# Head of a fused layernorm, state-space and SwiGLU kernel: other queues for the first loads, gate matmuls by halves of K

## The chip, the cores and the metric

The kernel runs on one core of one Trainium2 chip. The metric is the device time of one execution in microseconds; for several runs the median is given. A core has five engines that run their own instruction streams and meet at semaphores: TensorE (PE, matrix multiplications into the accumulator memory PSUM), VectorE (DVE), ScalarE (ACT), GpSimd (POOL) and SyncE (SP). Transfers between device memory and on-chip memory are done by 16 DMA engines. Here they are issued from two queues, SyncE's and ScalarE's.

## The reference

The input x has 2048 rows of 512 values in bfloat16. Each row is normalized to mean 0 and variance 1, and the result feeds two branches that are added to x:

```python
xn = _layernorm(x, axis=-1)
return x + _A_ref(xn, ...) + _B_ref(xn, B_w_gate, B_w_up, B_w_down)

# A: a diagonal complex recurrence along the rows, P = 512 states
dt = exp(log_dt); Lam_bar = exp(dt * Lam)
Bu = xn @ (((Lam_bar - 1) / Lam)[:, None] * Bmat).T
h = Lam_bar * h + Bu[t]                     # for every row t
y = 2 * Re(hseq @ Cmat.T) + xn * Dskip

# B: SwiGLU, F = 1376
(silu(xn @ w_gate) * (xn @ w_up)) @ w_down
```

## The kernel before

The 2048 rows are cut into 16 tiles of 128 rows, and four tiles make a chunk of 512 rows. Matmuls need xn with its columns on the partitions. For chunk 0 that transpose is done by TensorE, tile by tile (`xt_tile_fine`), and ScalarE copies the result from PSUM to `xnT`. Chunks 1 to 3 are transposed by a DMA on SyncE's queue (`xt_chunk_dma`).

For each chunk TensorE does the gate and up projections in pairs of 128-column tiles (`ffn_gate`, `ffn_up`, matmuls in line 713), the state-space input (`ssm_b_chunk`, line 818), and later the down projection together with the output of the recurrence in one accumulation (`dc_chunk`, lines 901 and 914). ScalarE empties PSUM with a silu (line 725) or a plain copy (lines 771 and 825). VectorE multiplies gate and up (line 773) and runs the recurrence (`ssm_elem_chunk`, lines 849 and 858). PSUM has eight banks, handed out in pairs in turn, so a matmul that starts a pair waits until ScalarE or VectorE has emptied it.

Everything is recorded as a task with what it reads and writes. A planner then orders each engine: TensorE's and SyncE's tasks keep the order in which they were recorded, while ScalarE, VectorE and GpSimd take what the planner's estimated durations and priorities make best. So a change in the head can reorder VectorE and ScalarE much later. An `order=` argument ties a task behind another without a wait.

The head works as follows. SyncE's queue loads x tiles 0, 1, 2, a slice of the gate weights (columns 512 to 767, all K), x tile 3, then the up weights, the rest of the gate weights, the rest of the up weights, and x tiles 4 to 7 in one load. ScalarE's queue loads log_dt (1 KB), the gate weights' columns 0 to 511 in two halves of K (`a0` and `a1`), then Lambda_im and Lambda_re (1 KB each). VectorE takes the statistics of a tile (line 466), aggregates them (470), adds epsilon (474); GpSimd raises to the power -1/2 (478); VectorE applies (485). Tile 0 is applied in two halves. TensorE meanwhile runs ten idle matmuls of 512 columns (`pe_warm`, line 450), then transposes tile 0 in two halves (543) with more idle matmuls between and after.

Then `ffn_gate_quarters` computes the gate projection of columns 0 to 767, six tiles in three PSUM pairs, one quarter of the chunk's rows (one x tile) at a time: 24 matmuls of 128 columns per quarter (line 752), each column tile with all four K parts at once, and only the very first one in two halves. The transposes of the next tile come between them. Three small transposes in line 457 turn the parameter rows into columns; they stand after the first eight gate matmuls.

Later SyncE's queue does, one after the other, the DMA transposes of B (real, imaginary), of xn's chunk 1, and of C (real, imaginary), and then loads x tiles 8 to 11, the down weights and the rest. The first transpose waits for all loads issued before it (line 380), and every load recorded after a transpose waits for that transpose. Chunk 2 is normalized on ScalarE (line 495), with a factor computed on VectorE (492).

Of the kernel before, what the change touches and what calls it, by code (L numbers as in the profile page):

```python
# [19 lines left out]
    warm=10,  # L20
# [218 lines left out]
def bass_parallel_sum__ssm_conv_s5__swiglu_ffn__prompt_kernel(  # L239
# [32 lines left out]
    with es:  # L272
# [46 lines left out]
        prow = sb("prow", [4, 3, 128], B16)  # L319
# [45 lines left out]
        def BK(b):  # L365
            return [("bk", b, 0), ("bk", b, 1)]
# [29 lines left out]
        def pload(name, slot, src, order=()):  # L396
            return dma(name, prow[:, slot, :], src.rearrange("(a p) -> a p", p=128), [("prow", slot)], 1024, eng="act", order=order)
        FQ = 4 * 128
        act_q = [pload("ld_ldt", 2, A_log_dt)]
# [6 lines left out]
        act_load("ld_wgA0", wg[:, 0:2, 0:FQ], wg_v[:, 0:2, 0:FQ], [("wg", "a0")], 256 * FQ * 2)  # L406
        dma("ld_x2", x_sb[:, 2:3, :], x_v[:, 2:3, :], [("x", 2)], TILEB)
        act_load("ld_wgA1", wg[:, 2:4, 0:FQ], wg_v[:, 2:4, 0:FQ], [("wg", "a1")], 256 * FQ * 2)
        dma("ld_wg0", wg[:, :, FQ:FH0], wg_v[:, :, FQ:FH0], [("wg", 0)], 512 * (FH0 - FQ) * 2)
        dma("ld_x3", x_sb[:, 3:4, :], x_v[:, 3:4, :], [("x", 3)], TILEB)  # L410
        act_q.append(pload("ld_lim", 1, A_Lambda_im, (act_q[-1],)))
        act_q.append(pload("ld_lre", 0, A_Lambda_re, (act_q[-1],)))
# [41 lines left out]
        def params_t(slot):  # L454
            def tr(e):
                for k in range(3):
                    inst = e.transpose(out=ptr[:, slot, 4 * k:4 * k + 4], in_=prow[0:4, k, :], identity=ident[0:4, 0:4])
                return inst
            g.add("pe", tr, reads=[("prow", k) for k in range(3)] + [("ident",)], writes=BK(slot), name="parT", est=100, ninst=3)
# [21 lines left out]
        def ln_apply(a, parts=1, order=()):  # L481
            w = D // parts
            for h in range(parts):
                cs = slice(h * w, (h + 1) * w)
                last = g.add("dve", lambda e, a=a, cs=cs: e.tensor_scalar(out=xn_sb[:, a % NXN, cs], in0=x_sb[:, a, cs], scalar1=mv[:, a, 0:1], scalar2=rstd[:, a:a + 1],
                                                                          op0=ALU.subtract, op1=ALU.mult),
                             reads=[("x", a), ("mv", a), ("rstd", a)], writes=([("xn", a % NXN)] if h == parts - 1 else []) + ([("xh", h)] if parts > 1 else []),
                             name="xn%d" % a, est=90 + 260 // parts, order=order)
            return last
# [10 lines left out]
        def ln_chunk0():  # L500
            bn_st(0)
            bn_ag(0)
            last = ln_ve(0, 1)
            ln_rstd(0, 1)
            last = ln_apply(0, parts=2, order=(bn_st(1, order=(last,)),))
            last = ln_ve(1, 1, order=(bn_ag(1, order=(last,)),))
            ln_rstd(1, 1)
            return bn_st(2, order=(last,))

        def ln_chunk0_rest(last, par_bank):  # L510
            last = ln_apply(1, order=(last,))
            for a in range(2, 4):
                last = ln_ve(a, 1, order=(bn_ag(a, order=(last,)),))
                hold[a] = ln_rstd(a, 1)
                if a == 2:
                    last = params_ev(par_bank, (last,))
                last = ln_apply(a, order=(bn_st(a + 1, order=(last,)),) if a < 3 else (last,))
# [15 lines left out]
        def xt_tile_fine(a, parts=1, wbank=None):  # L533
            n = KT // parts
            for h in range(parts):
                if h:
                    pe_warm(1, 256, wbank)
                slot = xt_pair[0] + (a + h) % 2

                def tr4(e, h=h, slot=slot):  # L540
                    for j in range(n):
                        kt = h * n + j
                        inst = e.transpose(out=ptr[:, slot, j * 128:(j + 1) * 128],
                                           in_=xn_sb[:, a % NXN, kt * 128:(kt + 1) * 128], identity=ident[:])
                    return inst
                g.add("pe", tr4, reads=([("xn", a % NXN)] if h == parts - 1 else []) + ([("xh", h)] if parts > 1 else []) + [("ident",)], writes=BK(slot), name="xT%d" % a, est=n * 64, ninst=n)

                def evac(e, h=h, slot=slot):
                    return e.activation(out=xnT[:, 0, a % 4, h * n:(h + 1) * n, :],
                                        in_=ptr[:, slot, 0:n * 128].rearrange("p (k t) -> p k t", k=n), func=AF.Identity)  # L550
                g.add("act", evac, reads=BK(slot), writes=([("xnT", 0, a % 4)] if h == parts - 1 else []) + ([("xnT0", h)] if parts > 1 else []), name="xTev%d" % a, est=190 + 310 // parts)
# [26 lines left out]
        def small(eng, name, fn, reads, writes, est=90):  # L578
            g.add(eng, fn, reads=reads, writes=writes, name=name, est=est, prio=_CFG['prio_par'])
# [40 lines left out]
        def params_b():  # L620
            dve_ts("thT", "thn", float(TP), ALU.mult)
            dve_range("thn")
            dve_range("thT")
            for i, n in enumerate(["lre", "lim"]):
                o = S(n)
                small("dve", n, lambda e, o=o, i=i: e.tensor_copy(out=o, in_=praw[:, i, :]), [("praw", i)], R(n))
            dve_tt("lam_re", "r", "cos_thn", ALU.mult)
            dve_tt("lam_im", "r", "sin_thn", ALU.mult)
            dve_ts("lm1", "lam_re", -1.0, ALU.add)
            dve_tt("lre2", "lre", "lre", ALU.mult)  # L630
            dve_tt("lim2", "lim", "lim", ALU.mult)
            dve_tt("den", "lre2", "lim2", ALU.add)
            o, a_ = S("rden"), S("den")
            small("dve", "rden", lambda e, o=o, a_=a_: e.reciprocal(out=o, in_=a_), R("den"), R("rden"))
            dve_tt("n1", "lm1", "lre", ALU.mult)
            dve_tt("n2", "lam_im", "lim", ALU.mult)
            dve_tt("n3", "n1", "n2", ALU.add)
            dve_tt("g_re", "n3", "rden", ALU.mult)
            dve_tt("n4", "lam_im", "lre", ALU.mult)
            dve_tt("n5", "lm1", "lim", ALU.mult)  # L640
            dve_tt("n6", "n4", "n5", ALU.subtract)
            dve_tt("g_im", "n6", "rden", ALU.mult)
            dve_ts("s_2gre", "g_re", 2.0, ALU.mult)
            dve_ts("s_m2gim", "g_im", -2.0, ALU.mult)
            dve_ts("s_m2gre", "g_re", -2.0, ALU.mult)
# [10 lines left out]
        def _tables():  # L656
            thn = S("thn")
            for pt in range(PT):
                b = pt % 2
                g.add("act", lambda e, pt=pt, b=b: e.activation(out=tm[:, b, :], in_=iot[:], func=AF.Identity, scale=thn[:, pt:pt + 1]),  # L660
                      reads=R("thn") + [("iot",)], writes=[("tm", b)], name="tm%d" % pt, est=620, prio=_CFG['prio_tab'])
# [35 lines left out]
        def wres(nm, i):  # L697
            if nm == "wg" and i < 4:
                return [("wg", "a0"), ("wg", "a1")]
            return [(nm, 0 if i < 6 else 1)]  # L700
# [34 lines left out]
        def ffn_gate_quarters(pairs, last):  # L735
# [3 lines left out]
            xt_tile_fine(0, parts=2, wbank=banks[pairs[-1]])  # L739
            pe_warm(3, 256, banks[pairs[-1]])  # L740
            tiles = [(2 * ip + k, banks[ip] + k) for ip in pairs for k in range(2)]
            for q in range(4):
                for ii, (i, bk) in enumerate(tiles):
                    if q == 0 and ii == 2:
                        params_t(tiles[-1][1])
                        ln_chunk0_rest(last, tiles[-1][1])
                    if q < 3 and ii == (4 if q == 0 else 2):
                        xt_tile_fine(q + 1)
                    for k0, k1 in (((0, 2), (2, 4)) if q == 0 and ii == 0 else ((0, 4),)):
                        def mm(e, bk=bk, i=i, q=q, k0=k0, k1=k1):  # L750
                            for kt in range(k0, k1):
                                inst = e.matmul(pbank[:, bk, q * 128:(q + 1) * 128], lhsT=wg[:, kt, i * 128:(i + 1) * 128], rhs=xnT[:, 0, q, kt, :],
                                                start=(kt == 0), stop=(kt == KT - 1))
                            return inst
                        xr = [("xnT", 0, q)] if q else [("xnT0", h) for h in range((k1 + 1) // 2)]
                        g.add("pe", mm, reads=wres("wg", i) + xr, writes=BK(bk), name="mm_gq%d_%d" % (i, q), est=(k1 - k0) * 56, ninst=k1 - k0)
# [170 lines left out]
        if _CFG["warm"]:  # L927
            pe_warm(_CFG["warm"])
        ffn_gate_quarters([0, 1, 2], ln_chunk0())
# [106 lines left out]
```

## Time and profile before

The median of four runs is 180.73 us (180.31 to 181.07). The profiled execution took 180.75 us, of which the span from the first to the last instruction is 179.0 us; the 1.75 us around it are outside the profile.

| | TensorE | VectorE | ScalarE | GpSimd |
|---|---|---|---|---|
| busy, us | 174.7 | 160.9 | 86.5 | 12.9 |
| share of the span | 98% | 90% | 48% | 7% |

| moment | us from the span's start |
|---|---|
| first idle matmul | 0.83 |
| statistics of x tile 0 begin | 2.90 |
| first transpose on TensorE | 5.18 |
| first gate matmul | 6.12 |
| first up matmul | 12.97 |
| x tiles 8 to 11, statistics begin | 41.43 |

Times are counted from the span's start. A row of the timeline or of the chain begins with a start and a length in microseconds; "x8" means that eight like instructions were merged. An engine's row can end with the idle time before it and what ended it. In the list of waits three numbers follow the pair: the total, how often, and the longest. "PEld" is the weight load of a matmul, which can run ahead of it.

### The profile page before, as it was taken

The page shows a single profiled execution, that of the slowest core. Times are in us where ns is not written, and L with a number is a line of the kernel's source. Part 1 is how long each engine was busy: PE and PEld are TensorE (multiplying, and loading weights), DVE is VectorE, ACT ScalarE, POOL GpSimd, SP SyncE. Part 2 cuts the span into 40 slices and gives each one's busy share as a digit, 9 for nine tenths or more (in the row PEclk, how much of TensorE's full clock was granted, in tenths as well). Part 3 has the DMA queues.
Part 4 walks back from the last instruction along what each step waited for, and adds up shares of the span by engine and source line. Part 5 has one row for each costly group of instructions (what it writes and reads, how often), then busy time and mean ns, then how long its engine had stood idle before and what let it go on. Part 6 is the DMA issues. An engine that isn't in the chain of part 4 may idle for free.

```text
span 179.0 us, 2380 instructions
## 1 busy us (share of the span) xinstructions
PE 174.7 (98%) x919; PEld 83.6 (47%) x927; DVE 160.9 (90%) x273; ACT 86.5 (48%) x107; POOL 12.9 (7%) x24
## 2 busy tenths in 40 slices
PE   8999999999999999999999999999999999999994
PEld 2694444444434444444444444444444444444743
DVE  3978759987799999999999999999999999999833
ACT  3379899899596992060655651000965620000000
POOL 3361300001400000210000000000000000000000
PEclk9999999999999999999999999999999999999999
DMA  5994546669450000002330000001100000001012
GB/s 153 355 352 89 110 87 126 109 151 359 149 111 10 0 0 0 0 0 89 79 72 0 0 0 4 0 0 59 59 0 4 0 0 0 0 0 62 29 59 88
DMA packets 23410, 12.37 MB, mean 69 GB/s; under 512 B 15112, under 2 KB 23400, under 8 KB 23400
## 3 DMA queue, kind: packets, MB, share of 16 engines
q1 hardware_dynamic: 22832, 11.70, 24.4%
q10 hardware_dynamic: 568, 0.53, 1.0%
q8 instruction: 7, 0.11, 0.3%
q14 instruction: 3, 0.02, 0.0%
HBM read 6.46 MB, written 2.10 MB: 48 GB/s over the span
## 4 chain that ended last, share of the span: by engine, by line
PE 70%; DMA 20%; SPq 2%; ACT 2%; DVE 2%; POOL 1%; issue 1%
PE pb L713 24%; PE pb L901 21%; PE pb L914 15%; PE pb L818 8%; DMA x_sb<-in_A_x_dram 7%; DMA BT<-in_A_B_im_dram 3%; DMA hss<-in_A_C_im_dram 3%; DMA BT<-in_A_B_re_dram 3%; DMA xnT<-xn_sb 2%; DMA hss<-in_A_C_re_dram 2%; SPq L385 2%; ACT xn_sb L495 2%; DVE st L466 1%; PE pb L781 1%; POOL rstd L478 1%
## 5 line engine op out<-in xcount | busy, mean ns | idle before, releaser
L858 DVE TENSOR_TENSOR_SCAN rot<-sm,car,rot 128x512 bf16<-128x512 f32 x32 | 39.0, 1265 | 0.1
L901 PE MATMUL pb<-wd,hT 128*128 128x512 bf16 (+3 forms) x194 | 38.1, 355 | 0.2
L713 PE MATMUL pb<-xnT,wu 128*128 128x512 bf16 x160 | 37.3, 379 | 0.4 <-ACT uf L771 0.4
L713 PE MATMUL pb<-xnT,wg 128*128 128x512 bf16 x136 | 32.0, 379 | 0.0
L914 PE MATMUL pb<-W,hss 128*128 128x512 bf16 (+2 forms) x140 | 28.1, 355 | 0.2
L818 PE MATMUL pb<-xnT,BT 128*128 128x512 bf16 x128 | 28.1, 379 | 0.0
L901 PEld LDWEIGHTS pb<-wd,hT 128*128 128x128 bf16 (+1 forms) x198 | 18.5, 98 | 19.9
L725 ACT ACTIVATE sg<-pb 128x1024 bf16<-128x1024 f32 x20 | 20.2, 1022 | 10.5 <-PE pb L713 10.4
L713 PEld LDWEIGHTS pb<-xnT,wu 128*128 128x128 bf16 x160 | 15.6, 98 | 19.3 <-ACT uf L771 0.9
L771 ACT ACTIVATE uf<-pb 128x1024 bf16<-128x1024 f32 x20 | 20.4, 1022 | 7.0 <-PE pb L713 6.8
L713 PEld LDWEIGHTS pb<-xnT,wg 128*128 128x128 bf16 x136 | 13.2, 98 | 16.4 <-issue 0.8
L914 PEld LDWEIGHTS pb<-W,hss 128*128 128x128 bf16 x144 | 13.5, 98 | 14.3
L818 PEld LDWEIGHTS pb<-xnT,BT 128*128 128x128 bf16 x128 | 12.5, 98 | 15.1
L825 ACT ACTIVATE u_sb<-pb 128x1024 bf16<-128x1024 f32 x16 | 16.3, 1027 | 3.9 <-PE pb L818 3.5
L466 DVE BATCH_NORM_STATS2 st<-x_sb 128x6 f32<-128x512 bf16 x16 | 10.2, 683 | 5.6 <-DMA x_sb<-in_A_x_dram 5.6
L773 DVE TENSOR_TENSOR hT<-sg,uf 128x1024 bf16<-128x1024 bf16 x20 | 13.3, 675 | 2.0 <-ACT uf L771 2.0
L919 DVE TENSOR_TENSOR x_sb<-pb,x_sb 128x512 bf16<-128x512 f32 (+2 forms) x18 | 10.9, 620 | 4.7 <-PE pb L914 4.7
L495 ACT ACTIVATE xn_sb<-x_sb,nmr,rstd 128x512 bf16<-128x512 bf16 x8 | 5.9, 803 | 10.8 <-DVE nmr L492 10.8
L800 ACT ACTIVATE sg<-pb 96x1024 bf16<-96x1024 f32 x2 | 2.0, 1020 | 17.4 <-PE pb L781 17.4
L849 DVE TENSOR_TENSOR rot<-rot,sin 128x2048 bf16<-128x2048 bf16 x8 | 9.7, 1214 | 0.0
L849 DVE TENSOR_TENSOR rot<-u_sb,sin 128x2048 bf16<-128x2048 bf16 x8 | 9.7, 1214 | 0.0
L849 DVE TENSOR_TENSOR rot<-u_sb,cosT 128x2048 bf16<-128x2048 bf16 x8 | 9.7, 1211 | 0.0
(71 smaller groups left out, 139.5 us busy)
## 6 DMA issues: line engine op xcount, KB each, us to landing
out_dram<-x_sb SPq DMA_DIRECT2D x15, 128.0 KB, 1.7
x_sb<-in_A_x_dram SPq DMA_DIRECT2D x3, 512.0 KB, 7.5
wd<-in_B_w_down_dram SPq DMA_DIRECT2D x1, 1280.0 KB, 7.0
wu<-in_B_w_up_dram SPq DMA_DIRECT2D x1, 768.0 KB, 6.2
wg<-in_B_w_gate_dram SPq DMA_DIRECT2D x1, 608.0 KB, 7.5
wu<-in_B_w_up_dram SPq DMA_DIRECT2D x1, 608.0 KB, 8.6
x_sb<-in_A_x_dram SPq DMA_DIRECT2D x4, 128.0 KB, 2.8
wg<-in_B_w_gate_dram ACTq DMA_DIRECT2D x2, 256.0 KB, 3.7
```

Source lines behind the costliest of these rows:

```text
L466: return g.add("dve", lambda e, a=a: e.bn_stats(out=st[:, a, :], in_=x_sb[:, a, :]), reads=[("x", a)], writes=[("st", a)], name="bnst%d" % ...
L713: inst = e.matmul(pbank[0:fs, bk, :].rearrange("p (j t) -> p j t", j=4), lhsT=w[:, kt, i * 128:i * 128 + fs], rhs=xnT[:, c % 2, :, kt, :], ...
L725: g.add("act", lambda e: e.activation(out=sg[rows, sl, 0:n, :].rearrange("p a t -> p (a t)"), in_=pair_f32(rows, bk, 512 * n), func=AF.Sil ...
L771: g.add("act", lambda e: e.activation(out=uf[rows, ul, 0:n, :].rearrange("p a t -> p (a t)"), in_=pair_f32(rows, bk, 512 * n), func=AF.Ide ...
L773: g.add("dve", lambda e: e.tensor_tensor(out=hT[rows, hb, i0:i0 + n, :], in0=sg[rows, sl, 0:n, :], in1=uf[rows, ul, 0:n, :], op=ALU.mult), ...
L818: inst = e.matmul(pbank[:, bk, :].rearrange("p (j t) -> p j t", j=4), lhsT=BT[:, ri, kt, pt * 128:(pt + 1) * 128], rhs=xnT[:, c % 2, :, kt ...
L825: g.add("act", lambda e: e.activation(out=u_sb[:, us].rearrange("p r t -> p (r t)"), in_=pair_f32(slice(0, 128), b0), func=AF.Identity), r ...
L849: tt = lambda out, a, b, op, r, w, nm: g.add("dve", lambda e: e.tensor_tensor(out=out, in0=a, in1=b, op=op), reads=r, writes=w, name="%s_% ...
L858: g.add("dve", lambda e, A0=A0, A1=A1, k=k, ri=ri, pt=pt: e.tensor_tensor_scan(out=A1[:, k, ri, :], data0=rr[:, pt:pt + 1].to_broadcast([1 ...
L901: inst = e.matmul(pbank[:, bk, 0:nc_], lhsT=hT[0:fs, hb, i, lt * 128:(lt + 1) * 128], rhs=wd[0:fs, i, c0:c0 + nc_], start=(i == 0), stop=F ...
L914: inst = e.matmul(pbank[:, bk, 0:nc_], lhsT=hss[:, hb, pt, ri, lt * 128:(lt + 1) * 128], rhs=W12[:, ri, pt, c0:c0 + nc_], start=False, sto ...
L919: g.add("dve", lambda e, bk=bk, a=a, c0=c0, nc_=nc_: e.tensor_tensor(out=x_sb[:, a, c0:c0 + nc_], in0=pbank[:, bk, 0:nc_], in1=x_sb[:, a, ...
```

## The change

On SyncE's queue x tiles 0 to 2 are followed by the two small loads of Lambda_im and Lambda_re and then by x tile 3; the slice of gate weights is gone from it. On ScalarE's queue log_dt is followed by two loads that hold the gate weights' columns 0 to 767, one per half of K. The parameter rows lie in 12 partitions instead of 4 by 3, so that one transpose serves them, and it moves between the two halves of tile 0's transpose.

Ten idle matmuls of 512 columns become 41 of 128. The idle matmul between the halves goes, and the three of 256 columns after them become two of 128. On VectorE the aggregate and epsilon of tile 1 come between the two halves of tile 0. All four tiles are now transposed and copied out in halves, and the gate matmuls run over all six column tiles with the first half of K and then with the second; in the last quarter only the first two tiles are halved. Small parameter work on ScalarE is held behind the last of these copies, and two small copies on VectorE behind the normalization of tile 3.

```diff
-        prow = sb("prow", [4, 3, 128], B16)
+        prow = sb("prow", [12, 128], B16)
...
+        def pload(name, slot, src, eng="sp"):
+            return dma(name, prow[4 * slot:4 * slot + 4, :], src.rearrange("(a p) -> a p", p=128), [("prow", slot)], 1024, eng=eng)
+        act_q = [pload("ld_ldt", 2, A_log_dt, "act")]
...
-        act_load("ld_wgA0", wg[:, 0:2, 0:FQ], wg_v[:, 0:2, 0:FQ], [("wg", "a0")], 256 * FQ * 2)
+        act_load("ld_wgA0", wg[:, 0:2, 0:FH0], wg_v[:, 0:2, 0:FH0], [("wg", "a0")], 256 * FH0 * 2)
         dma("ld_x2", x_sb[:, 2:3, :], x_v[:, 2:3, :], [("x", 2)], TILEB)
-        act_load("ld_wgA1", wg[:, 2:4, 0:FQ], wg_v[:, 2:4, 0:FQ], [("wg", "a1")], 256 * FQ * 2)
-        dma("ld_wg0", wg[:, :, FQ:FH0], wg_v[:, :, FQ:FH0], [("wg", 0)], 512 * (FH0 - FQ) * 2)
+        act_load("ld_wgA1", wg[:, 2:4, 0:FH0], wg_v[:, 2:4, 0:FH0], [("wg", "a1")], 256 * FH0 * 2)
+        pload("ld_lim", 1, A_Lambda_im)
+        pload("ld_lre", 0, A_Lambda_re)
         dma("ld_x3", x_sb[:, 3:4, :], x_v[:, 3:4, :], [("x", 3)], TILEB)
-        act_q.append(pload("ld_lim", 1, A_Lambda_im, (act_q[-1],)))
-        act_q.append(pload("ld_lre", 0, A_Lambda_re, (act_q[-1],)))
...
-                for k in range(3):
-                    inst = e.transpose(out=ptr[:, slot, 4 * k:4 * k + 4], in_=prow[0:4, k, :], identity=ident[0:4, 0:4])
+            g.add("pe", lambda e: e.transpose(out=ptr[:, slot, 0:12], in_=prow[:], identity=ident[0:12, 0:12]),
...
+        def ln_chunk0(par_bank):
+            last = stats(1, hold["last"])
+            last = ln_half(0, 1, order=(last,))
+            last = params_ev(par_bank, (last,))
+            last = bn_st(2, order=(last,))
+            last = ln_apply(1, order=(last,))
...
+            small(...): order=(hold["evac"],) if eng == "act" else ()
...
-            xt_tile_fine(0, parts=2, wbank=banks[pairs[-1]])
-            pe_warm(3, 256, banks[pairs[-1]])
+            pe_warm(41, 128, wbank)
+            ln_first()
+            xt_tile_fine(0, bridge=bridge)      # bridge: params_t, ln_chunk0
+            pe_warm(2, 128, wbank)
             for q in range(4):
+                if q < 3:
+                    steps = [(i, bk, 2 * kh, 2 * kh + 2) for kh in range(2) for i, bk in tiles]
+                else:
+                    steps = [(i, bk, 2 * kh, 2 * kh + 2) for kh in range(2) for i, bk in tiles[:2]] + [(i, bk, 0, 4) for i, bk in tiles[2:]]
+                for n, (i, bk, k0, k1) in enumerate(steps):
+                    if q < 3 and n == 8:
+                        xt_tile_fine(q + 1)
...
-        if _CFG["warm"]:
-            pe_warm(_CFG["warm"])
-        ffn_gate_quarters([0, 1, 2], ln_chunk0())
+        ffn_gate_quarters([0, 1, 2])
```

## The prediction

> **What bounds the kernel now.** I read the busy shares first (TensorE 98%, VectorE 90%), then the chain that ended last, then who waited for whom. TensorE looks like the bound everywhere, so anything saved in its first 13 us should come out at the end. The chain, in order of time (start, length, what), says otherwise:
>
> ```profile
> 4.89 9.36 DMA x_sb<-in_A_x_dram
> ...
> 14.64 4.59 DMA BT<-in_A_B_re_dram
> ...
> 19.25 5.50 DMA BT<-in_A_B_im_dram
> ...
> 24.77 4.25 DMA xnT<-xn_sb
> ...
> 29.04 4.20 DMA hss<-in_A_C_re_dram
> ...
> 33.26 4.60 DMA hss<-in_A_C_im_dram
> ...
> 37.88 3.53 DMA x_sb<-in_A_x_dram
> ...
> 41.43 2.47 DVE st L466 x4
> ...
> 47.01 2.93 ACT xn_sb L495 x4
> 49.94 0.92 ACT uf L771
> ...
> 50.91 8.81 PE pb L713 x40
> ```
>
> Up to 50.9 us the end hangs on SyncE's queue: tiles 4 to 7 of x are the last of the initial loads, the first transpose waits for all of these, five transposes follow one another, then tiles 8 to 11 are loaded, normalized on VectorE, GpSimd and ScalarE, and only then does ScalarE copy out the bank that TensorE wants. From 50.91 on TensorE runs without a wait: 179.0 - 50.9 = 128.1 us. The waits (in total, times, longest) show the meeting point:
>
> ```profile
> PEld pb L713 <- ACT uf L771: 0.9, 1, 0.9
> PE pb L713 <- ACT uf L771: 0.4, 1, 0.4
> ```
>
> TensorE arrives there 0.4 us early. A head that ends earlier only lengthens this wait; one that ends up to 0.4 us later costs nothing. The head itself, TensorE alone:
>
> ```profile
> 5.18 0.37 PE L543 MATMUL pb<-ident,xn_sb 128*128 128x128 bf16 x2
> ...
> 6.12 0.69 PE L752 MATMUL pb<-xnT,wg 128*128 128x128 bf16 x8
> 6.75 0.22 PE L457 MATMUL pb<-ident,prow 4*128 4x4 bf16 x3
> ...
> 8.44 0.62 PE L752 MATMUL pb<-xnT,wg 128*128 128x128 bf16 x8 [0.24 <-ACT xnT L549]
> ...
> 9.12 1.50 PE L752 MATMUL pb<-xnT,wg 128*128 128x128 bf16 x24
> ...
> 12.97 4.26 PE L713 MATMUL pb<-xnT,wu 128*128 128x512 bf16 x19
> ```
>
> From 6.12 to 12.97 are 6.85 us. Spacing is (1.50 - 0.22)/23 = 0.056, so 96 gate matmuls and 12 transposes take 6.05; 0.8 is waits and the parameter transposes.
>
> Last, the load stream in quarter microseconds (TensorE, weight loads, VectorE, ScalarE, GpSimd, clock, DMA share, GB/s), with 512-byte rows (the wg slice) and 1536-byte rows (wu):
>
> ```profile
> 5.50:5.75 0.25, 0.25 (x5) 0.21 (x4) 0.25 (x2) 0.16 (x1) 0.10 (x1) 1.00 1.09 317
> 8.75:9.00 0.25, 0.25 (x8) 0.25 (x6) 0.22 (x3) 0.00 (x0) 0.25 (x1) 1.00 1.08 393
> ```
>
> The engines are full in both; longer rows move more.
>
> **What the Trainium skill says.** "DMA: Bandwidth & Descriptors", section Queues, rings and completion order: each DMA engine takes packets in turn from the queues that have work, so a load on ScalarE's queue shares the engines with SyncE's. The trace agrees that they share, but not evenly in the short run: from 4.00 to 4.25 SyncE's queue moved 0.05 MB and ScalarE's 0.02, from 4.75 to 5.00 0.00 and 0.08. The same page, Why small descriptors are slow: a fixed overhead per packet; 317 against 393 GB/s agrees. "TensorE: Matmul & The Clock Gate", What's actually happening: the clock rises after about 3.4 us of activity, in a free-running window. Here 512-wide idle matmuls are 0.43 apart, and the clock record has full speed from 5.5, 4.7 us after the first. The same page, Architectural detail: VectorE is strictly in order, so what stands behind a waiting instruction waits too; its order below matters for that.
>
> **Part by part.** *Idle matmuls.* 41 of 128 columns are 5248 columns against 5120: at 0.43 per 512, 4.4 us, ending at 5.2 as before. Nothing, since the first half of tile 0 is normalized only at 5.04. At equal activity the clock should rise at the same time.
>
> *Parameters.* One transpose for three, now between the two halves of tile 0 and so ahead of all gate matmuls. Lambda_im and Lambda_re go from ScalarE's queue to SyncE's, behind x2. On the old queue their last landing events were 0.35 and 0.74 us after that of the load ahead of them (5.90, then 6.25 and 6.64). x2 landed at 1.72 + 3.3 = 5.0; so Lambda_re lands at about 5.75, bounds 5.3 and 6.6. VectorE now does tile 1's aggregate and epsilon between the halves of tile 0, so half two is normalized at 5.6 (before 5.3), which this wait hides. Transposes at 5.8 to 6.0, two idle matmuls, first gate matmul at 6.1, as before. The parameter copy stands on VectorE ahead of x2's statistics: tile 1 is normalized at 7.2 instead of 6.7; its transposes come only after 16 gate matmuls, at 7.3.
>
> *Gate weights.* ScalarE's queue carries 786 KB instead of 524. It had moved its 524 by 5.3 us; 262 KB more take 0.8 us if it gets nearly everything (346 GB/s at 4.75) and 1.55 at half; with the 0.6 from last data to landing seen on the old load, 6.7 to 7.4. I take 7.0. The 12 matmuls on the first K half end at 6.1 + 0.67 = 6.8: a wait of 0.2.
>
> *Halves.* The copy of each tile becomes two (0.38 each, 0.28 apart, against 0.60), and 8 matmuls cover it: 0.45 against 0.53 needed, some 0.08 left per tile; the 0.41 before tile 1's matmuls goes. Sum: 7.0 + 84 x 0.056 + 12 x 0.056 + 0.3 = 12.7. The up projection begins 0.2 us earlier (12.3 to 13.5 over both bounds). TensorE then waits 0.6 instead of 0.4 at 50.9. Worth nothing; without that cover it would be worth the 0.2.
>
> *Load stream.* This moves the end. No bytes change, but 256 KB in 512-byte rows become 1536-byte ones: 262/317 - 262/393 = 0.16 us less. The other 524 KB go from 1024-byte rows (346) to 393: at most 0.18 more, in a stretch where the engines were not yet full, so perhaps nothing. Against it SyncE issues two small loads (0.38 + 0.35) for one slice (0.44), so later issues come 0.3 us later; ScalarE's longer backlog covers that; uncovered it costs 0.3. Net -0.2, bounds -0.34 and +0.3. Every later link shifts by the same.
>
> *Order after.* Built, the changed program has the same TensorE order from the up projection on, and ScalarE still has silu, four normalizations, then the awaited copy. VectorE's order changes: statistics of tiles 8 to 11 now stand ahead of one table operation (0.68) and two scans (1.2 each). It idles for that load with 3.0 us of work behind it, and has hardly a free moment until 169. The last h was ready at 165.6 and is first used at 169.7: 4.1 of margin become about 1.2; W (69.9, used at 76.0) keeps 3. Free as long as this cover holds.
>
> Sum against the profiled execution: 179.0 - 0.2 = 178.8 span; that run took 180.75, the median is 180.73, so 180.5 us. A difference below 0.3% (0.54 us) can hardly be told from no change.
>
> **Rivals.** *Faster, by the loads.* Both row gains come in full (0.34), and the engines' free share from 2.0 to 4.5 us (0.3 us in sum) is filled by ScalarE's longer rows: -0.64, 180.1. For it: shares of 0.66 to 0.78 up to 2.75. [...]
>
> *Slower, by the second K half.* All six tiles wait for it, so the up projection begins at 12.7 + (landing - 7.0), and the end is 179.0 + (that start - 12.97 - 0.42) once the cover at 50.9 is used up: no loss against before up to a landing at 7.7, 0.3% from 8.25. With a third of the stream (320/3 = 107 GB/s) the last 262 KB take 2.45 us: landing at 5.3 + 2.45 + 0.6 = 8.35, up projection at 14.05, +0.66: 181.4. Lambda_re landing past 6.6 would act in the same place. For it: SyncE's queue holds long rows right behind x3. Against it: ScalarE's queue had over half from 2.75 to 5.25.
>
> *Slower, by VectorE.* A lag of over 4.1 us makes the last down projection wait; at 5 it is 181.4. Against: the 3.0 above.
>
> *No cover at 50.9*, the head's whole 0.8 arriving at the end, would need this wait to be absent, and the chain denies it.
>
> **Numbers.** Forecast, end tied to the load stream: 0.60, nearly all of it within 0.3%. Faster by the loads 0.17; late K half 0.13; VectorE 0.06; the rest unknown, 0.04, put to slower. Faster 0.19, same 0.58, slower 0.23. The forecast's own range is 180.4 to 181.0; taking in the nearer part of the outer cases, 180.0 to 181.4.
>
> **What would show it.** Right: x's second load (512 KB) landing within 0.35 us of 14.25 and the awaited L771 copy shifted by as much; up projection between 12.3 and 13.5; wait at L713 on L771 of 0.4 to 1. Wrong: no such wait (the head is late), gate matmuls waiting for the weights beyond 7.7, a cold clock past 6 us, or TensorE waiting for VectorE near 170.

## The result, and the profile after

The changed kernel takes 182.05 us, the median of 43 runs (180.48 to 183.87), against 180.76 for the kernel before (64 runs, 180.23 to 181.46): a ratio of 1.0058, with an interval of 1.0046 to 1.007. That ratio doesn't count the one run at 183.87, far above the others, and isn't one of medians, which would give 1.0071. The changed kernel is slower, where no change was forecast, and the median lies outside the range of 180.0 to 181.4. The profiled execution took 181.48 with a span of 179.7; before, the span was 179.0.

The chain that ended last, after (start, length, what):

```profile
2.60 4.29 DMA prow<-in_A_Lambda_re_dram
...
6.98 0.16 PE pb L453
...
7.48 0.89 PE pb L760 x16
...
13.95 12.09 PE pb L713 x56
...
49.25 1.41 ACT xn_sb L485 x2
50.66 0.92 ACT uf L780
51.62 8.81 PE pb L713 x40
```

Where SyncE's loads and transposes stood, the 1 KB load of Lambda_re now begins the chain, and TensorE's head follows it. The meeting point has moved from 50.91 to 51.62, and these 0.71 us are the whole difference of the spans. The waits after, in the parts that answer to those shown of before (total, times, longest):

```profile
PE pb L453 <- DMA prow<-in_A_Lambda_re_dram: 1.5, 1, 1.5
...
PEld pb L713 <- ACT uf L780: 0.8, 1, 0.8
...
PE pb L713 <- ACT uf L780: 0.3, 1, 0.3
```

The head on TensorE, from the timeline after:

```profile
5.20 0.27 PE L542 MATMUL pb<-ident,xn_sb 128*128 128x128 bf16 x2
6.98 0.16 PE L453 MATMUL pb<-ident,prow 12*128 12x12 bf16 x1 [1.51 <-DMA prow<-in_A_Lambda_re_dram]
...
7.32 1.05 PE L760 MATMUL pb<-xnT,wg 128*128 128x128 bf16 x16
...
11.86 2.09 PE L760 MATMUL pb<-xnT,wg 128*128 128x128 bf16 x32
13.79 2.54 PE L713 MATMUL pb<-xnT,wu 128*128 128x512 bf16 x11
```

The parameter transpose waits 1.51 us for Lambda_re, which lands at 6.89, and every gate matmul is queued behind it. From the first gate matmul to the up projection it is 6.47 us, less than the 6.85 of before; but it starts at 7.32 instead of 6.12, so the up projection starts 0.82 later.

That is not yet all, since a wait at 51 us is left: the other arm is late too. VectorE's and then ScalarE's timeline after:

```profile
15.42 2.47 DVE L461 BATCH_NORM_STATS2 st<-x_sb 128x6 f32<-128x512 bf16 x4 [1.75 <-DMA x_sb<-in_A_x_dram]
...
42.15 2.47 DVE L461 BATCH_NORM_STATS2 st<-x_sb 128x6 f32<-128x512 bf16 x4 [2.53 <-DMA x_sb<-in_A_x_dram]
```

```profile
47.73 2.93 ACT L485 ACTIVATE xn_sb<-x_sb,nmr,rstd 128x512 bf16<-128x512 bf16 x4 [1.69 <-DVE nmr L482]
50.56 1.00 ACT L780 ACTIVATE uf<-pb 128x1024 bf16<-128x1024 f32 x1
```

x tiles 4 to 7 arrive 1.15 us later than before (their last landing event is at 15.40 instead of 14.25), tiles 8 to 11 at 42.15 instead of 41.43 (0.72 later, since the loads and transposes between took 0.43 us less this time), and ScalarE, which from 47.73 on is never idle, comes to the awaited copy 0.71 later. The chain leads from that copy to TensorE because a TensorE event happens to end at 49.25 too; ScalarE's row shows that it was waiting for nothing then. So two arms, each some 0.7 to 0.8 us late, meet at 51.6.

The windows of the load stream after (TensorE, weight loads, VectorE, ScalarE, GpSimd, clock, DMA share, GB/s):

```profile
5.50:5.75 0.25, 0.00 (x0) 0.00 (x0) 0.09 (x1) 0.24 (x1) 0.25 (x1) 1.00 0.88 275
...
8.75:9.00 0.25, 0.25 (x8) 0.24 (x5) 0.25 (x1) 0.25 (x2) 0.25 (x1) 1.00 1.07 389
```

In the first of them TensorE is idle, and VectorE, whose next instruction is the parameters' copy, nearly so. The runs differ in one thing more: in 11 of 43 timed runs the mean granted clock is 0.991, and these took 182.1 to 182.9. In the 184 runs of before that were taken beside the experiments it is 0.999 or more.

Why do two loads of 1 KB take until 6.89? The DMA queues of the changed kernel from 5.0 to 5.5 us (packets, MB, share of 16 engines), in the trace's view of the transfers:

```profile
q10 hardware_dynamic: 112, 0.17, 115.4%
```

This is ScalarE's queue, and SyncE's moved nothing in that half microsecond: x2 had landed at 5.25, Lambda_im and Lambda_re stood next, and the 786 KB of gate weights had the engines.

And why is the end of the x load late? The same view from 12.5 to 14.0 us:

```profile
q1 hardware_dynamic: 256, 0.25, 51.7%
q8 instruction: 1, 0.02, 4.7%
```

One packet of 16 KB of instructions, 4.7% of 24 engine-microseconds or 1.1 us on a single engine. It came at 12.76, while x was still being loaded; before, at 13.44, when the load was nearly done. Of the load's 16 landing events 15 had come by 14.34; the last alone came at 15.40. Three of the experiments below with narrow idle matmuls show the same: 15 events by 14.42, the last at 15.49 to 15.50. Which engine carried the packet is not in the trace, so that it was the late one is inferred. 31 more idle matmuls, each with its weight load, are 62 more instructions on TensorE. "Runtime: NRT & Kernel Launch" of the Trainium skill, section Instruction fetch mechanics, says that instructions are fetched in blocks of 16 KiB, 256 instructions, over a DMA queue, and that this is mostly hidden. The trace agrees with the size; that it is hidden depends on what the engine has to carry at the time.

### The profile page after: what moved, and what is told of

It reads as the page before. It is cut to its first block, busy times and chain, and to the rows that moved or that the text cites. A ratio compares the mean times of both kernels' runs of the same rounds, so it can differ in the third digit from the quotient of the medians.

```text
span 179.7 us, 2438 instructions
## 1 busy us (share of the span) xinstructions
PE 174.3 (97%) x946; PEld 86.2 (48%) x954; DVE 160.3 (89%) x273; ACT 86.4 (48%) x110; POOL 12.2 (7%) x24
## 4 chain that ended last, share of the span: by engine, by line
PE 93%; DMA 2%; ACT 1%; SPq 1%; issue 0%; DVE 0%
PE pb L713 35%; PE pb L910 21%; PE pb L827 15%; PE pb L923 15%; PE pb L760 3%; DMA prow<-in_A_Lambda_re_dram 2%; PE pb L790 2%; PE pb L800 1%; SPq L384 1%; ACT xn_sb L485 1%; PE pb L542 1%; ACT uf L780 1%; DVE x_sb L928 0%; PE pb L453 0%; PE pb L448 0%
## 5 line engine op out<-in xcount | busy, mean ns | idle before, releaser
L713 PEld LDWEIGHTS pb<-xnT,wg 128*128 128x128 bf16 x136 | 13.2, 98 | 16.4 <-issue 0.8
L827 PEld LDWEIGHTS pb<-xnT,BT 128*128 128x128 bf16 x128 | 12.5, 98 | 15.1
L858 DVE TENSOR_TENSOR rot<-rot,cosT 128x2048 bf16<-128x2048 bf16 x8 | 9.7, 1213 | 0.0
```

The source lines that it names most:

```text
L713: inst = e.matmul(pbank[0:fs, bk, :].rearrange("p (j t) -> p j t", j=4), lhsT=w[:, kt, i * 128:i * 128 + fs], rhs=xnT[:, c % 2, :, kt, :], ...
L827: inst = e.matmul(pbank[:, bk, :].rearrange("p (j t) -> p j t", j=4), lhsT=BT[:, ri, kt, pt * 128:(pt + 1) * 128], rhs=xnT[:, c % 2, :, kt ...
L858: tt = lambda out, a, b, op, r, w, nm: g.add("dve", lambda e: e.tensor_tensor(out=out, in0=a, in1=b, op=op), reads=r, writes=w, name="%s_% ...
```

## Experiments

Each ratio is to runs of the kernel before on the same chip, which had medians of 180.58 to 180.70. "Late parameters" is the theory that the wait for Lambda_re is the loss; "fetch" that the end of the x load is.

**Parameters ahead of the gate weights.** On ScalarE's queue, log_dt, Lambda_im, Lambda_re, then the two halves:

```
-        pload("ld_lim", 1, A_Lambda_im)
-        pload("ld_lre", 0, A_Lambda_re)
+        for nm_, sl_, src_ in (("ld_lim", 1, A_Lambda_im), ("ld_lre", 0, A_Lambda_re)):
+            act_q.append(pload(nm_, sl_, src_, "act"))
```

> The changed kernel, with Lambda_im and Lambda_re loaded on ScalarE's queue between log_dt and the gate weights, so that they land near 3 us. Late-parameter theory (the parameter transpose waited 1.5 us for Lambda_re, which made the head late): the wait goes, the up projection begins at 12.4 to 13.1 instead of 13.8, and the end falls to or below that of before, 180.3 to 180.8. Instruction-fetch theory (one 16 KB fetch of TensorE's instructions sits on one DMA engine at 12.8 us, while that engine still has part of x tiles 4 to 7, and makes the whole chain of transposes late): the fetch stays and comes earlier, x tiles 4 to 7 still land near 15.3, x tiles 8 to 11 near 42.1, and the end stays at 181.2 to 181.6. In both the runs with a low mean clock should go, if the idle 1.5 us caused them.

184.55 (6 runs), ratio 1.0213 [1.0161, 1.0265]. Both theories missed. The parameters are transposed at 5.51 without a wait, but a new wait takes the place: the two halves of the gate weights land at 7.26 and 9.36. Its timeline and then its windows:

```profile
7.40 0.83 PE L761 MATMUL pb<-xnT,wg 128*128 128x128 bf16 x12 [1.33 <-DMA wg<-in_B_w_gate_dram]
9.49 0.58 PE L761 MATMUL pb<-xnT,wg 128*128 128x128 bf16 x4 [1.26 <-DMA wg<-in_B_w_gate_dram]
```

```profile
5.80:9.00 3.20, 1.10 (x16) 0.78 (x14) 2.50 (x9) 0.58 (x2) 0.81 (x3) 1.00 1.02 351
9.25:12.50 3.25, 3.01 (x29) 3.04 (x30) 2.28 (x18) 0.66 (x2) 2.20 (x3) 0.50 1.07 373
```

In 3.2 us TensorE is busy for 1.10, and for the next 3.4 (9.18 to 12.59 in the clock record) the clock is 0.50: the 24 gate matmuls that take 1.59 elsewhere take 2.60. Five of the six runs have a mean clock of 0.99. That is what the 0.991 of the changed kernel's longer runs comes to: half of 3.4 us is 0.9% of the span.

**Wide idle matmuls.** In the changed kernel:

```
-            pe_warm(41, 128, wbank)
+            pe_warm(10, 512, wbank)
```

> The changed kernel with ten idle matmuls of 512 columns instead of 41 of 128, 62 TensorE instructions fewer. Instruction-fetch theory: the fetch comes about 1.5 us later, after the load stream, x tiles 4 to 7 land at 13.9 to 14.3 and tiles 8 to 11 near 41.2; the head stays late by 0.8, 0.4 beyond the cover, so about 181.2. Late-parameter theory alone: nothing changes in the landings, 182.0.

181.77 (22 runs), ratio 1.0048 [1.003, 1.0066]; 6 of the 22 at a mean clock of 0.991. The fetch is at 13.57 and x tiles 4 to 7 land at 14.19, as the fetch theory says, but only 0.1% comes back: the wait for Lambda_re is still there (1.03), and the up projection starts at 13.92. The load chain gains less than it should, too. x tiles 8 to 11 come at 41.79, not near 41.2, for the transpose of C real takes 5.81 instead of 4.31 us; the next block of instructions now falls into it, at 31.66.

**Both of these edits.**

> The changed kernel with both edits: parameters first on ScalarE's queue, and ten wide idle matmuls. If the two causes together are all, the end returns to the forecast: up projection at 12.4 to 13.1, x tiles 4 to 7 landing at 13.9 to 14.3, 180.4 to 180.7, no runs with a low clock. If something else costs, 181 or more.

182.70 (6 runs), ratio 1.0106 [1.0071, 1.0141]: missed. The second half of the gate weights is waited for by 1.7 us, and a window at half clock follows as in the first experiment.

**Narrow idle matmuls in the kernel before.**

```
-            pe_warm(_CFG["warm"])
+            pe_warm(41, 128)
```

> The kernel before with 41 idle matmuls of 128 columns instead of ten of 512, and nothing else. Instruction-fetch theory: the fetch moves from 13.4 to below 12.7, into the load stream; x tiles 4 to 7 land at 14.8 to 15.4 instead of 14.25, and the end is 0.5 to 1.1 later, 181.3 to 181.9. Late-parameter theory: no change, 180.8.

181.46 (16 runs), ratio 1.0053 [1.0032, 1.0074]. The edit alone costs half a per cent, with nothing moved in the queues; the fetch theory's 181.3 to 181.9 is met. Its one profiled execution, at 183.48, lies far above the median and is not read.

**Parameters on SyncE's queue ahead of x2**, in the changed kernel:

```
+        pload("ld_lim", 1, A_Lambda_im)
+        pload("ld_lre", 0, A_Lambda_re)
         dma("ld_x2", ...)
```

> The changed kernel with Lambda_im and Lambda_re moved on SyncE's queue from behind x tile 2 to ahead of it; ScalarE's queue and all later issues keep their times. Late-parameter theory: Lambda_re lands at about 5 us instead of 6.9, the parameter transpose no longer waits, gate matmuls begin near 6.1 and wait 0 to 0.8 for the second K half, the up projection begins at 12.5 to 13.2, and no run loses a clock window; if that was the whole loss, 180.5 to 180.8. With the fetch theory on top (fetch at about 12 us, inside the load stream), x tiles 4 to 7 land near 15 and it stays at 181.2 to 181.6.

180.80 (14 runs), ratio 1.0017 [1.0002, 1.0031], no run at low clock. Lambda_re lands at 5.45, gates begin at 6.09; x2 lands at 7.23, and its transposes wait 0.85, so the up projection still starts at 13.79, not at 12.5 to 13.2:

```profile
6.09 1.37 PE L760 MATMUL pb<-xnT,wg 128*128 128x128 bf16 x16
8.32 0.40 PE L542 MATMUL pb<-ident,xn_sb 128*128 128x128 bf16 x4 [0.85 <-DVE xn_sb L477]
```

In this profile x tiles 4 to 7 land late (15.50), but the transposes take less, tiles 8 to 11 land at 40.75 and nobody waits at 51 us, so 179.2 is the head alone. With the wait ahead of the gates gone, the half clock is gone too.

**The same with wide idle matmuls.**

> The same with ten idle matmuls of 512 columns, so that the instruction fetch comes about 1.6 us later. Both theories together: 0.2 to 0.8 faster than the run without this edit, 180.4 to 180.8, with the wait at the up projection's bank near 50 us at 0.6 or more. If the late half of the gate weights is what remains, the up projection begins past 13.5 and the time stays above 181.

180.93 (22 runs), ratio 1.0021 [1.0008, 1.0033]. x tiles 4 to 7 land at 14.56 instead of 15.50, the up projection starts at 13.35, and no time is gained: a miss of the fetch theory's sizes.

**x tiles 8 to 11 ahead of both transposes of C**, in the kernel before: the load moves up by two places in `loads_stage_b2`.

> The kernel before with one load moved: x tiles 8 to 11 ahead of the two transposes of C instead of behind them. If the end hangs on the chain of transposes up to 50.9 us, as the prediction said, the 0.4 us wait there goes and the end comes 0.4 to 0.6 earlier, 180.0 to 180.3. If the wait is only a by-product, no change.

180.57 (14 runs), ratio 0.9994 [0.9982, 1.0005]. No gain. In its profile there is no wait on ScalarE at 51 us, as expected, but the head is late:

```profile
7.37 0.62 PE L752 MATMUL pb<-xnT,wg 128*128 128x128 bf16 x8 [0.96 <-DMA wg<-in_B_w_gate_dram]
...
14.08 2.11 PE L713 MATMUL pb<-xnT,wu 128*128 128x512 bf16 x9
```

Its span of 179.5 is 165.4 more than 14.08.

**Parameters ahead of x2, wide idle matmuls, x tiles 8 to 11 between the transposes of C.**

> The changed kernel with parameters ahead of x tile 2, ten wide idle matmuls, and x tiles 8 to 11 loaded between the two transposes of C. If the changed head is really earlier once its two side effects are gone, and only the chain hides it, the end is 0.3 to 0.7 below the same kernel without the moved load: 179.8 to 180.3. If the head is no earlier than before, 180.5 or more.

180.65 (22 runs), ratio 1.0004 [0.9991, 1.0017]: level with before. The head is what ends last, since x2 is still waited for (0.78).

**Parameter transpose behind tile 0's gate matmuls**, loads as changed:

```
             def bridge():
-                params_t(pbk)
-                ln_chunk0(pbk)
+                ln_chunk0()
...
+                    if q == 1 and n == 0:
+                        params_t(pbk)
+                        params_ev(pbk, (hold["xn2"],))
```

> The changed kernel with the parameter transpose moved from between tile 0's halves to behind the 24 gate matmuls of tile 0 (its copy on VectorE behind the normalization of tile 2); loads and queues stay as changed, so Lambda_re lands at about 6.9 as before. Theory 'late Lambda_re ahead of the gates is the loss': nobody waits for it any more, the first gate matmul is at 5.9 to 6.3, the second K half lands at 6.7 to 7.2, the up projection begins at 12.6 to 13.0, the clock is full in every run, median 180.3 to 180.9. Rival 'the loss is elsewhere in the change' (end of the x loads at 15.4 instead of 14.25, statistics ahead of table work on VectorE, copies in halves): the gates start early and the median is still 181.4 or more.

181.25 (7 runs), ratio 1.0034 [1.0021, 1.0048]. The gates begin at 5.96, but the bank that the parameters were transposed into is wanted again before VectorE has copied it, and TensorE waits 0.90 for that: the up projection starts at 13.92. A wait of my own making, so that this run can't tell the theories apart. With a head this late, but the clock full in all runs and nobody waiting at 51 us in the profile, the runs take 180.97 to 181.5.

**The same with wide idle matmuls.**

> The same with ten idle matmuls of 512 columns instead of 41 of 128, so that the 16 KB instruction fetch falls behind the initial loads again. Fetch theory: x tiles 4 to 7 land at 14.0 to 14.6 instead of 14.6 to 15.5, and with an early head the loads are what ends last, so 0.3 to 0.8 faster than with narrow ones: 180.0 to 180.4. Rival 'the loads do not end last in most runs': within 0.3 of the run with narrow ones.

181.13 (22 runs), ratio 1.0021 [1.0009, 1.0033]. The same wait (1.2), the head at 13.89; the fetch makes no difference as long as the head is that late.

**Lambda_im and Lambda_re on SyncE's queue behind x2, in the kernel before.**

```
-            ... 1024, eng="act", order=order)
+            ... 1024, eng="act" if slot == 2 else "sp", order=order)
```

> The kernel before with one edit: Lambda_im and Lambda_re on SyncE's queue behind x2 instead of behind ScalarE's gate weights. The parameter transposes stay behind the first eight gate matmuls. Theory 'it is the place ahead of the gates, not the queue': Lambda_re lands between 5.6 and 6.9, the wait at the parameter transpose is at most 0.3, the median stays within 0.5 of before, 180.3 to 181.1. Rival 'small loads on SyncE's queue push back what follows': gate slice and x3 land 0.3 or more later, up projection at 13.4 or later, median 181.3 or more.

180.64 (14 runs), ratio 1.0 [0.9989, 1.0012]. With ScalarE's shorter queue Lambda_re lands at 6.07, and the transposes at 6.67 find it there:

```profile
6.67 0.22 PE L457 MATMUL pb<-ident,prow 4*128 4x4 bf16 x3
...
13.20 2.97 PE L713 MATMUL pb<-xnT,wu 128*128 128x512 bf16 x13
```

The new queue costs nothing by itself; the place ahead of the gates, with the longer loads on the other queue, does. As an estimate, a landing at 6.07 would still have made TensorE, idle from 5.48 in the changed kernel, wait some 0.6 us at that place.

**The second of these runs with x tiles 8 to 11 between the transposes of C.**

> The second of these runs with x tiles 8 to 11 loaded between the transposes of C real and C imaginary. If the load chain ends last there, this takes its slack away and gives 179.9 to 180.3, which would beat both kernels; if the head or VectorE ends last, within 0.2 of the second run.

181.61 (6 runs), ratio 1.0052 [1.0034, 1.007]: missed, and slower than without. With x early, ScalarE takes two of the four normalizations ahead of an earlier copy (L812), for which TensorE waits 0.45 at 46.6; that this is the 0.5 lost was not tested.

**Parameter transpose behind tile 1's gate matmuls**: `q == 2` in the edit above, and the copy ordered behind the normalization of tile 3.

> The changed kernel with the parameter transpose behind the gate matmuls of tile 1, its copy on VectorE behind the normalization of tile 3; loads as changed. Theory 'late Lambda_re ahead of the gates': neither the parameters nor their copy is waited for by more than 0.2, gates start at 5.9 to 6.3, the up projection begins at 12.7 to 13.2, the clock is full in every run, and the median is 180.3 to 180.8. Rival 'half the loss is elsewhere' (the x load's end at 15.4 because of the instruction fetch, VectorE's order): with that early head still 181.1 or more.

181.04 (14 runs), ratio 1.002 [0.9992, 1.0048], all at full clock, between what the two theories gave. Now no parameter wait is left, and the head is as the prediction had it:

```profile
6.11 1.10 PE L761 MATMUL pb<-xnT,wg 128*128 128x128 bf16 x16
...
12.71 3.62 PE L712 MATMUL pb<-xnT,wu 128*128 128x512 bf16 x16
```

But eight runs lie at 179.9 to 181.2 and six at 181.7 to 182.3. The profiled one (182.04) is of the second kind. Its waits, and VectorE's row for x tiles 8 to 11:

```profile
PE pb L712 <- ACT uf L781: 1.4, 1, 1.4
```

```profile
42.63 2.47 DVE L461 BATCH_NORM_STATS2 st<-x_sb 128x6 f32<-128x512 bf16 x4 [3.00 <-DMA x_sb<-in_A_x_dram]
```

With the head mended, the other arm shows: x tiles 4 to 7 landed at 15.49, with an instruction packet at 11.20.

**The same with wide idle matmuls.**

> The same with ten idle matmuls of 512 columns. With an early head the loads should end last: fetch theory gives 0.3 to 0.8 less than with narrow ones, 180.0 to 180.3. Rival 'what ends last lies elsewhere': within 0.2 of it.

180.87 (22 runs), ratio 1.0011 [0.9994, 1.0028]. Two runs of 22 are above 181.6 instead of six of 14; x tiles 4 to 7 land at 14.66. The median moves by 0.17 only, against 0.3 to 0.8 expected. What is left at 51 us is a wait of 0.3.

**And with x tiles 8 to 11 between the transposes of C.**

> The second with x tiles 8 to 11 loaded between the transposes of C real and C imaginary. If the load chain ends last: 0.3 or more below the second, 179.7 to 180.1, a version that beats both kernels. If not, because VectorE or PSUM banks end last once x8 is early: within 0.2 of the second, or slower as VectorE takes the statistics ahead of its tables.

180.33 (22 runs, 179.69 to 181.81), ratio 0.9976 [0.9963, 0.9989]. This is 0.54 less than the second, where 0.3 or more was expected, though not as low as 179.7 to 180.1. It is faster than both kernels, over before by a quarter of a per cent, less than the 0.3% below which single kernels can hardly be told apart here. Its chain has no load after the first one; the head runs straight into the rest:

```profile
13.09 12.09 PE pb L712 x56
...
41.70 17.40 PE pb L712 x80
```

**Read together.** Span less start of the up projection:

| kernel | up projection | span | difference | TensorE's wait for ScalarE near 51 us |
|---|---|---|---|---|
| before | 12.97 | 179.0 | 166.0 | 0.4 |
| after | 13.79 | 179.7 | 165.9 | 0.3 |
| parameters ahead of x2 | 13.79 | 179.2 | 165.4 | none |
| before, x tiles 8 to 11 early | 14.08 | 179.5 | 165.4 | none |
| before, parameters on SyncE | 13.20 | 178.7 | 165.5 | none |
| parameters mid gates | 12.71 | 180.3 | 167.6 | 1.4 |
| the same, wide | 13.27 | 179.2 | 165.9 | 0.3 |
| the same, wide, x tiles 8 to 11 early | 12.93 | 178.4 | 165.5 | none |

Where the loads are not waited for, the span is 165.4 to 165.5 us more than the start of the up projection; in all ten profiles without that wait it is 165.4 to 165.7. So the end is the later of two: head + 165.45, or the load chain. For the profiled run after, the head alone gives 179.24, and the loads make 179.7 of it; with the head of before the loads would still make 179.7, and with the loads of before the head would still leave about 179.2. In that one execution, undoing one of the two would show little. In the medians the parameters weigh more: 181.77 with the fetch moved, 181.04 (in two groups) with the parameters moved, 180.87 with both. The interval of the last, 0.9994 to 1.0028, includes no change.

## Why the prediction was wrong

*What bounds the kernel.* Half right. The mechanism, a head and a load chain that meet at 51 us, fits the profiles of both kernels. But one execution of before was taken for all: its head was early. In the run with x8 early, which has the same head, the gates waited 0.96 us for their weights and the up projection began at 14.08 instead of 12.97. The median span in the run with x8 early, 180.57 - 1.75 = 178.8, less 165.45 gives an up projection at about 13.35, an estimate from the rule above. So the cover of 0.4 was probably that run's; the experiment that loads x tiles 8 to 11 earlier in before gained nothing.

*Idle matmuls.* Costed at nothing, because the columns are the same. As work on TensorE this is right: they end at 5.2. What was left out is that they are instructions, and that instructions are fetched by the same DMA engines. In the kernel before the edit alone is +0.5%.

*Parameters.* This step failed, and most of the loss comes from it: with the parameters out of the way and nearly all else as changed, the ratio falls from 1.0058 to 1.002, and to 1.0017 where only their place in SyncE's queue was moved. Lambda_re was put at 5.75 with bounds 5.3 and 6.6; it landed at 6.89. The lag of 0.35 and 0.74 behind the load ahead had been measured on ScalarE's queue at a time when that queue was not competing with a longer one; behind x2 (5.25, predicted 5.0) it was 1.27 and 1.64. It was no accident of one execution: in the eight profiles with these loads Lambda_re lands at 6.27 to 7.02, about when the second half of the gate weights does (6.58 to 7.23), and in four past the bound of 6.6. In the kernel before with the same place in SyncE's queue and ScalarE's shorter loads, the two land at 6.07 and 5.66. The step on the gate weights, a few lines further on, gives ScalarE's queue nearly all of the engines up to 5.3 us and beyond. The two were not put together: the bandwidth that makes one load early makes the other late. The transpose stood ahead of all gate matmuls, so of these 1.14 us the up projection saw most: it was due at 12.7 and started at 13.79.

*Clock.* Not foreseen at all for this place. "At equal activity the clock should rise at the same time" is right for the rise: the first gate matmuls already come 0.055 us apart. But the wait ahead of them leaves TensorE idle for 1.5 us, and in a quarter of the runs, to judge by their mean clock, a window at half clock follows. The Trainium skill, "TensorE: Matmul & The Clock Gate", What's actually happening, has the clock fall back after an idle window of about 3.4 us. The trace agrees with the length of 3.4 us, but in the first experiment the window before held 1.10 us of matmuls in 3.2, and in the third 1.66 in 3.4, so a wholly idle one isn't needed.

*Gate weights and halves.* Right. The second half of K landed at 6.70 (7.0, bounds 6.7 to 7.4), and gates to up projection took 6.47, where 12.7 - 6.1 = 6.6 was predicted. That the forecast wait of 0.2 for the second half is missing is the late start's doing. With the parameters mid gates the head runs from 6.11 to 12.71, just as predicted.

*Load stream.* -0.2, bounds -0.34 and +0.3; measured +1.15 at x tiles 4 to 7, mostly because of the fetch. With the wide idle matmuls they land at 14.19, 0.06 earlier than before: most of the 0.2 that the row lengths were to bring doesn't show.

*Order after.* Right: the last h is ready at 169.1 and first used at 170.3, the predicted margin of 1.2, and TensorE waits for it nowhere.

*Rivals.* "Lambda_re landing past 6.6 would act in the same place" names what happened, inside the rival of a late second half, with the right place; its formula gives 13.79 - 12.97 - 0.42 = 0.40 of the 0.71, the rest being the loads. Its chance of 0.13 was for another load. None of the signs of being right came: the x load was off by 1.15, past the 0.35, the awaited copy moved by 0.71 and not by as much, the up projection began at 13.79 and the wait was 0.3. Of the signs of being wrong the profile shows none; a cold clock past 6 us fits the quarter of the runs at a lower mean clock.

What stays open: why, with the parameters out of the way, the narrow idle matmuls make six of 14 runs long and not all, and why the median gains only 0.17 without them. A likely reason for the second, not tested: the wide ones take one block of instructions out of the x load but put the next into the transpose of C real (see the last section). The other links of the load chain vary as well (4.00 to 5.86 us for the transpose of B imaginary), and only one execution of each kernel was looked into. The profiled execution after, 181.48, is also one of the shorter ones: of the further 0.57 to the median, the half clock explains a part (the median of the runs at full clock is about 181.6), and the rest wasn't seen. The moved parameters change VectorE's order a little too, so that run isn't quite one edit.

## What to carry to other kernels

A small load took as long here as the queue in front of it and the other queue's bulk made it: ask which queue has the engines in the microsecond in which it is due, and put what waits for it behind work that doesn't. Where two arms meet, undoing one shows only what it has over the other, so cost both before and read more than one execution of each to know which is later. Count instructions as traffic when the DMA engines are full.

## What the hardware showed that was not expected

- A block of 16 KB of instructions took about 1.1 us of one DMA engine. Where it met the end of a load that is spread over all 16, one of the 16 parts landed later: 15.40 instead of 14.19 us with the same bytes.
- The transpose of C real took 4.06 to 4.31 us in the nine profiles where no block of instructions begins in it, or only within 0.15 us of its ends. It took 4.79 to 5.99 in the eight where a block begins in its midst, between 29.80 and 31.66 us, all of them with wide idle matmuls. In the wide version with the parameters mid gates it was 5.64, with a block at 31.49. This was seen, not tested.
- A window in which TensorE was busy for a third of the time, in another run for half of it, was followed by half clock over the next 3.4 us: 24 matmuls of 128 columns in 2.60 instead of 1.59 us.
- ScalarE's queue alone filled the engines for half a microsecond (0.17 MB, SyncE's nothing), although Lambda_im and Lambda_re waited at the head of SyncE's.
